# Gate and value products by Strassen's seven products for eight, with streamed weight sums, in a hashed attention and gated unit kernel

## The chip, the core and the metric

The kernel runs on one core of a Trainium2 chip. The metric is the device time of one execution in microseconds (us). It is 1079.8 us (median of three runs, 1078.91 to 1079.8) before the change. The core has five engines that run side by side, each through its own instructions in order: PE (TensorE, matrix products, whose results go to PSUM banks), DVE (VectorE), ACT (ScalarE), POOL (GpSimd) and SP, which here issues nearly all DMAs.

## The reference

```python
def _attn_ref(q, k, v, proj):                      # q, k, v: (4, 8, 768, 64)
    q_bits = (np.einsum('bhsd,dk->bhsk', q, proj) > 0).astype(np.int64)
    k_bits = (np.einsum('bhsd,dk->bhsk', k, proj) > 0).astype(np.int64)
...
    mask = q_bucket[:, :, :, None] == k_bucket[:, :, None, :]
    scores = np.where(mask, scale * np.matmul(q, k.transpose(0, 1, 3, 2)), -1000000000.0)
    attn = np.exp(scores - np.max(scores, axis=-1, keepdims=True))
    attn = attn / (np.sum(attn, axis=-1, keepdims=True) + 1e-09)
    return np.matmul(attn, v)

def _moe_ref(x, w_gate, w_val, w_out):             # x: (3072, 512); 512x1536, 512x1536, 1536x512
    gate = 1.0 / (1.0 + np.exp(-(x @ w_gate)))
    return gate * (x @ w_val) @ w_out
```

The output of the attention, with its heads side by side, is the `x` of the gated unit. The three weights come as 64-bit floats and are made into pairs of 32-bit numbers (a high part and a low part) on the chip.

## The kernel before

Every product of full precision is three matmuls: low by high, high by low, high by high. The tokens are eight units `(b, g)` of `GN` = 384 tokens: four batches, two halves each. The columns of gate and value are twelve blocks `j` of 128, the 512 rows of a weight four chunks `c`. One block of one unit takes 12 matmuls of 128x384 for the gate (tile `zg`), 12 for the value (`zv`), and then 9 matmuls of 128x512 into the three output tiles of the unit (`zo`, `yo`).

There are two stages. In the **attention stage** 16 pairs of heads go through scores (`sc`, L722 and L727), maximum (L736), exponential (L755), transposes (`tp`, L788), copies (`ef`, L795) and values (`pv`, L805); the result is stored to DRAM as `xd` (L818). Between these pieces PE does blocks 0 to 2 (`J1` = 3) of the six units of batches 0 to 2 (`moe_early`). At the same time 30 of the 36 weight blocks are loaded as raw 64-bit words and converted by DVE, ACT and POOL (`load_w`); 21 of them go back to DRAM (`kept`). When the last `xd` is stored, the task `switch` frees the attention's memory, and the **late stage** (`moe_late`) has all weights in SBUF: first batch 3 with all twelve blocks, then the other six units with blocks 3 to 11. A unit's `x` is loaded (`xr`) and split into `xh` (ACT) and `xl` (POOL or DVE); there is one buffer for it (`x=1`), so the split of the next unit waits for the last value product of the one before.

All instructions are tasks of a planner (`Plan`). It has a duration for each task, hands out buffers by counts (`stock`), and writes each engine's order down; on the chip each engine then goes through its order and waits only for data and buffers. A DMA's landing is planned as 2000 ns and 1 ns for 200 bytes, up to eight in flight without a common rate; the transfers after `switch` are planned with `CROWDED` = 1,600,000 bytes each in place of their own.

Of the kernel before, what the change touches and what calls it, by code (L numbers as in the profile page):

```python
# [169 lines left out]
def lsh_attention_glu_kernel(ctx, tc, q, k, v, proj, w_gate, w_val, w_out, out):  # L170
# [12 lines left out]
    J1 = 3  # L183
    J2 = 10
# [55 lines left out]
    hw = {}  # L240
    ALL = range(P // HB)
    for n, signs, groups in (("q", (1.0, -1.0), ALL), ("k0", (-1.0, 1.0), ALL[::2]), ("k1", (-1.0, 1.0), ALL[1::2])):
        w = const.tile([P, P], F32, name=f"hw{n}", tag="hw")
# [28 lines left out]
    def busy():  # L272
# [26 lines left out]
    def load_w(key, n, j, early, last=None):  # L299

        z = {}
        stage = lambda: later["w"] if last else stage1

        def load():
            z["raw"] = raw = stage().tile([P, 2 * N_EL], I32, name=f"raw{n}{j}", tag="wraw", bufs=2 if last else 1)
            if n == "o":  # L310
                nc.sync.dma_start(raw, w_out[j * P : (j + 1) * P, :])
            else:
                w = w_gate if n == "g" else w_val
                nc.sync.dma_start(
                    raw.rearrange("p (c f) -> p c f", c=KC),
                    w[:, 2 * j * P : 2 * (j + 1) * P].rearrange("(c p) f -> p c f", p=P),
                )
# [26 lines left out]
        def scaled(eng):  # L344
            eng.tensor_mul(f(z["ex"]), f(z["mf"]), f(z["ex"]))

        def high():
            if early or last:
                z["w"] = (w1 if early else stage()).tile([P, 2, N_EL], F32R, name=f"w{n}{j}", tag=f"w{n}{j}")
                weights[n, j] = z["w"][:, 0], z["w"][:, 1]  # L350
            else:
                z["w"] = stage1.tile([P, 2, N_EL], F32R, name=f"w{n}{j}", tag="wk", bufs=stock["wk"])
            nc.scalar.copy(z["w"][:, 0], f(z["ex"]))
# [580 lines left out]
```

## Time and profile before

| | us |
|---|---|
| median of three runs | 1079.8 |
| span of the profiled execution | 1077.3 |
| PE busy | 1056.2 (98%) |
| DVE busy | 556.1 (52%) |
| ACT busy | 493.0 (46%) |
| POOL busy | 261.1 (24%) |
| first late product | 579.0 |

The span is the time from the first to the last instruction. A matmul's busy time overlaps the next one's, since matmuls are pipelined; what one costs is the distance from its start to the start of the next. The profiled execution has no time of its own but its span; the median of the runs is 2.5 us above that span.

### The profile page before, as it was taken

To read this page: it belongs to the slowest core of one execution; us is meant where nothing else is said; L and a number is where in the kernel's file an instruction comes from. 1 tells how busy PE (TensorE), PEld (TensorE's weight loads), DVE (VectorE), ACT (ScalarE), POOL (GpSimd) and SP (SyncE) were. 2 spreads that over 40 slices of the span, in tenths; PEclk is the share of its full clock that TensorE was granted. 3 is DMA by queue.
4 is the path that set the end of the run, shared out by engine and by line. 5 is a ranking of instruction groups with operands and counts; after the bars stand their busy time and mean duration, and the time that the engine had idled before them with its cause. 6 is when DMAs were issued, how large, how long until landed. Compare 5 with 4: busy or idle time off the path is not lost.

```text
span 1077.3 us, 20491 instructions
## 1 busy us (share of the span) xinstructions
PE 1056.2 (98%) x8409; PEld 845.2 (78%) x8412; DVE 556.1 (52%) x1188; ACT 493.0 (46%) x887; POOL 261.1 (24%) x238
## 2 busy tenths in 40 slices
PE   9999999999999999999999999999999999999998
PEld 5665566677676776676678999999999999999997
DVE  6899899968788788788751181011021202020201
ACT  2867677767586676767652132112121212121211
POOL 0013233313324132323012172112121212121211
PEclk9999999999999999999999999999999999999999
DMA  8345545554664456443126621002020202020000
GB/s 206 84 125 159 148 148 138 160 162 129 197 199 127 156 154 192 149 143 135 56 61 248 267 80 59 1 1 88 1 88 1 89 1 89 1 83 6 31 28 30
DMA packets 110846, 113.54 MB, mean 105 GB/s; under 512 B 60320, under 2 KB 92064, under 8 KB 110752
## 3 DMA queue, kind: packets, MB, share of 16 engines
q1 hardware_dynamic: 110592, 112.23, 33.8%
q8 instruction: 66, 1.08, 0.4%
q14 instruction: 28, 0.23, 0.1%
q10 hardware_dynamic: 160, 0.00, 0.0%
HBM read 70.78 MB, written 28.84 MB: 92 GB/s over the span
## 4 chain that ended last, share of the span: by engine, by line
PE 83%; DVE 6%; ACT 4%; POOL 3%; DMA 2%; issue 2%; SPq 0%; POOLq 0%; DVEq 0%; ACTq 0%
PE pv L805 10%; PE sc L722 8%; PE zv_0l L429 8%; PE zv_1l L429 7%; PE zg_0l L429 7%; PE zg_1l L429 7%; PE yo_0l L462 7%; PE yo_1l L462 7%; PE tp L788 5%; PE zg L429 4%; PE zv L429 3%; PE zo L462 3%; PE sc L727 2%; DVE e L736 2%; ACT e L755 2%
## 5 line engine op out<-in xcount | busy, mean ns | idle before, releaser
L755 ACT ACTIVATE e<-e,st 128x768 f32<-128x768 f32 x192 | 196.4, 1025 | 81.2 <-DVE st L748 81.2
L736 DVE TENSOR_SCALAR_CACHE_REDUCE e<-sc 128x768 f32<-128x768 f32 x192 | 177.8, 952 | 34.9 <-PE sc L727 33.6
L805 PE MATMUL pv<-ef,vr 128*64 128x384 f32 x768 | 141.5, 497 | 0.0
L445 DVE TENSOR_TENSOR gf_1l<-zv_1l,sig 128x384 f32<-128x384 f32 x39 | 21.8, 558 | 208.6 <-PE zv_1l L429 208.6
L445 DVE TENSOR_TENSOR gf_0l<-zv_0l,sig 128x384 f32<-128x384 f32 x39 | 21.7, 557 | 189.8 <-PE zv_0l L429 189.8
L788 PEld LDWEIGHTS tp<-ident,e 64*128 64x128 f32 x2304 | 83.7, 139 | 30.5 <-issue 15.2
L795 DVE COPY ef<-tp 128x768 f32<-128x768 f32 x90 | 84.9, 951 | 26.1 <-PE tp L788 26.0
L788 PE MATMUL tp<-ident,e 64*128 64x64 f32 x2304 | 94.7, 226 | 2.4 <-ACT ef L795 1.0
L722 PE MATMUL sc<-kh,ql 64*128 64x384 f32 x192 | 86.2, 449 | 6.0 <-DVE ql L650 2.1
L795 ACT COPY ef<-tp 128x768 f32<-128x768 f32 x102 | 79.6, 792 | 25.3 <-PE tp L788 24.9
L805 PEld LDWEIGHTS pv<-ef,vr 128*64 128x64 f32 x768 | 47.8, 136 | 52.9 <-issue 46.5
L722 PE MATMUL sc<-kh,qsl 64*128 64x384 f32 x192 | 86.2, 449 | 3.1 <-ACT ef L795 1.1
L429 PE MATMUL zg_1l<-xh_1l,wg 128*128 128x384 f32 x312 | 86.4, 337 | 0.0
L429 PE MATMUL zg_0l<-xh_0l,wg 128*128 128x384 f32 x312 | 86.4, 337 | 0.0
L429 PE MATMUL zv_1l<-xh_1l,wv 128*128 128x384 f32 x312 | 85.5, 334 | 0.0
L429 PE MATMUL zv_0l<-xh_0l,wv 128*128 128x384 f32 x312 | 85.5, 334 | 0.0
L450 POOL TENSOR_TENSOR gl<-gf_1l,gh 128x384 fp32r<-128x384 f32 x39 | 40.5, 1039 | 184.5 <-ACT gh L449 184.5
L815 POOL TENSOR_TENSOR xs<-xs,rb 128x384 f32<-128x384 f32 x32 | 33.2, 1037 | 202.3 <-DVE xs L812 155.8
L450 POOL TENSOR_TENSOR gl<-gf_0l,gh 128x384 fp32r<-128x384 f32 x37 | 39.7, 1072 | 162.0 <-ACT gh L449 162.0
L462 PE MATMUL yo_0l<-wo,gh 128*128 128x512 f32 x234 | 73.5, 395 | 0.0
L462 PE MATMUL yo_1l<-wo,gh 128*128 128x512 f32 x234 | 73.5, 395 | 0.0
L581 ACT ACTIVATE sig<-zg_1l 128x384 f32<-128x384 f32 x39 | 19.2, 492 | 115.8 <-PE zg_1l L429 115.8
(160 smaller groups left out, 2495.0 us busy)
## 6 DMA issues: line engine op xcount, KB each, us to landing
kr<-in_k_dram SPq DMA_DIRECT2D x64, 96.0 KB
qr<-in_q_dram SPq DMA_DIRECT2D x32, 192.0 KB
vr<-in_v_dram SPq DMA_DIRECT2D x16, 384.0 KB
qsh<-qh SPq DMA_DIRECT2D x32, 192.0 KB
qsl<-ql SPq DMA_DIRECT2D x32, 192.0 KB
rb<-rd SPq DMA_DIRECT2D x64, 96.0 KB
xd<-xs SPq DMA_DIRECT2D x32, 192.0 KB
rawg<-in_moe_w_gate_dram SPq DMA_DIRECT2D x12, 512.0 KB
```

The source lines that it names most:

```text
L429: nc.tensor.matmul(z["acc"][:, :GN], a[:, wc], x[xx][:, c, :], start=(c == 0 and i == 0), stop=(c == KC - 1 and i == 2),)
L445: nc.vector.tensor_mul(z["gf"], z["acc"][:, :GN], sig[:, j])
L450: low = lambda eng: eng.tensor_sub(gl[:, j], z["gf"], f(gh[:, j]))
L462: nc.tensor.matmul(acc, a[:, slot, ts_], w, start=(first and i == 0), stop=(last and i == 2))
L722: nc.tensor.matmul(sc[:, j, :GN], q_[rows, c], z["k" + x][rows, h * GN : (h + 1) * GN], start=(m == 0), stop=False, tile_position=(j * D, 0),)
L727: nc.tensor.matmul(sc[:, j, :GN], z["qb"][rows, c], z["kb"][rows, h], start=False, stop=True, tile_position=(j * D, 0),)
L736: nc.vector.tensor_scalar(sp(e), gz["sc", t, h][:, :, :GN], -SCALE, None, op0=ALU.mult, op1=ALU.min, accum_out=gz["st", t][:, 0, h : h + 1],)
L755: nc.scalar.activation(e, e, AF.Exp, bias=st[:, 2, h : h + 1], scale=st[:, 1, h : h + 1], accum_out=gz["su"][:, h * GT + t : h * GT + t + 1],)
L788: nc.tensor.transpose(tp[:, r, at_ : at_ + D], gz["e", t, h][rows, c * P : (c + 1) * P], ident[rows, rows], tile_position=(r * D, 0),)
L795: copy(gz["ef", c].rearrange("p (n r d) -> p r n d", r=2, d=D), gz["tp", c][:, :, :GN].rearrange("p r (n d) -> p r n d", d=D),)
L805: nc.tensor.matmul(gz["pv"][rows, :GN], z["v"][:, h, c], gz["ef", c][:, h * GN : (h + 1) * GN], start=(c == 0), stop=(c == NC - 1), tile_p ...
L815: nc.gpsimd.tensor_mul(gz["xs"], gz["xs"], gz["rb"])
```

## The change

Gate and value columns are taken in pairs of blocks `jp`, and a whole batch (two units) at once. Of a pair, the two blocks of columns, the two halves of the 512 rows, and the two units of tokens make a 2x2 by 2x2 product, which Strassen's scheme (in Winograd's form) does with seven products in place of eight. `visit` is one gate or one value of one pair for one batch: seven times six matmuls of 128x384, in the order m1, m2, m6, m5, m7, m4, m3, in two PSUM banks. Bank B is read by ACT after m1, m6 and m7 while PE waits to add the next product to it (`copied`, tiles `t1`, `t16`, `t167`), and DVE adds those to the other bank (`summed`).

- The sums and differences of weights (`S1`, `S2`, `S3`, `S4`) are made once (`load_pair`), split, and kept in DRAM with the plain blocks: seven slices, two chunks and two parts, 1.835 MB for a visit. Each visit fetches them (`fetch_stream`) into one of three slots. The pairs 4 and 5 are converted in the late stage during the first batch.
- The sums of `x` are made at the beginning of each batch: tiles `x0` to `x6`, 128x768 each, with four differences (L649 of the changed kernel, tiles `rx` and `xb`), seven high parts on ACT (L654) and seven low parts (L657). Each has one buffer, released by the last visit of the batch before.
- The early blocks are now two (`J1` = 2), and all eight units do them; those of batch 3 come after the last `xd`, ahead of the visits. Ten of twelve blocks are in visits: 4 batches x 5 pairs x 2 = 40 visits.
- The output products of a pair are six pieces of six 128x512 matmuls; three go into each of the next two visits (`fill`).
- Each transfer is planned with its own size; `CROWDED` is unused.

```diff
-    J1 = 3
-    J2 = 10
+    J1 = 2
+    J2 = 8
+    JP1, JP2, JPN = J1 // 2, J2 // 2, NJ // 2
...
+    WS = 3
+    late_stock = dict(y=6, t=3, zt=3, xt0=1, xt1=1, ws1=1, ws2=1, xb=1, x1=1, x4=1, x5=1, x6=1)
...
+        def sums(eng):
+            y["f"] = full = f(z["all"]).rearrange("p (s m) -> p s m", s=SL)
+            at_ = lambda s_: full[:, s_]
+            eng.tensor_add(at_(S1), at_(A21), at_(A22))
+            eng.tensor_sub(at_(S2), at_(S1), at_(A11))
+            eng.tensor_sub(at_(S3), at_(A11), at_(A21))
+            eng.tensor_sub(at_(S4), at_(A12), at_(S2))
...
+        h0 = highs("x0", here("x0"), [l0])
+        t1 = differences("x4", "xt0", b12, here("x0"), [l0, lb])
+        ready["x0"] = lows("x0", here("x0"), [h0, t1])
+        t2 = differences("x5", "xt1", b22, diff("x4"), [t1])
+        h4 = highs("x4", diff("x4"), [t1], ["x4"])
+        ready["x4"] = lows("x4", diff("x4"), [h4, t2], ["xt0"])
+        t4 = differences("x6", "xt0", here("x1"), diff("x5"), [t2, l1, ready["x4"]])
+        h1 = highs("x1", here("x1"), [l1])
+        ready["x1"] = lows("x1", here("x1"), [h1, t4])
...
+            def mm(bank, a_, x_, first, last):
...
+                for c in range(2):
+                    for i, (wa, xa) in enumerate(((1, 0), (0, 1), (0, 0))):
+                        nc.tensor.matmul(
+                            acc, streams[n, jp][:, c, wa, a_], X[x_][:, xa, c],
+                            start=first and c == 0 and i == 0, stop=c == 1 and i == 2,
+                            skip_group_check=not first or not last,
+                        )
...
+            prev = m1 = m(prev, "B", A11, "x0", True, False, take=["one"], give=used("xr"))
+            e1 = copies("t1", m1)
+            prev = m2 = m(prev, "A", A12, "x1", True, True, take=["one"], give=used("x1"))
+            c11 = sum_(0, "A", "t1", [m2, e1], ["one", "t"])
+            prev = fill(prev)
+            prev = m6 = m(prev, "B", S2, "x5", False, False, [e1], give=used("x5"))
+            e16 = copies("t16", m6)
+            prev = m5 = m(prev, "D", S1, "x4", True, False, take=["one"], give=used("x4"))
+            prev = m7 = m(prev, "B", S3, "x2", False, False, [e16])
+            e167 = copies("t167", m7)
+            c22 = sum_(3, "D", "t167", [m5, e167], ["t"])
+            prev = fill(prev)
+            prev = m4 = m(prev, "B", A22, "x6", False, True, [e167], give=used("x6"))
+            prev = m3 = m(prev, "D", S4, "x3", False, True, [c22, *held], give=[slot_[1]] + used("x"))
+            c12 = sum_(1, "D", "t16", [m3, e16], ["one", "t"])
+            prev = fill(prev)
...
+        slots["last"] = dma(
+            1e3 + slots["n"], 1835008, fetch, after=[later["switch"], slots["last"], *keeps[n, jp]], take=[slot[1]]
+        )
...
-        made[w] = dma(1e3, CROWDED, fetch, after=[a, later["switch"]])
...
+        made[w] = dma(1e3 + w[1] * 2 - 2.5, 524288, fetch, after=[a, later["switch"]])
+    ends = dict(first=True, s=None, turn=0, pieces=[], sides=[dict(h=gh, l=gl, free=g_free[J1 - 1]), dict(free=None)])
+    prev = later["switch"]
+    for b in range(B):
+        prev = products(2e4 + b, b, prev, ends)
```

Where the stages meet, SP's order before was this (`xr` are the loads of `x`, `wg`, `wv`, `wo` the kept weights, `part` the stores of early sums):

```order
L818 DMA xd_65<-xs_3_1_8877 128x384
L364 DMA wg_8927<-kg_102 128x1024
L392 DMA xr_1l<-xd_65 128x4x384
L513 DMA part_100<-ob_2_1_8929 128x512
L364 DMA wv_8940<-kv_109 128x1024
L364 DMA wo_8948<-ko_116 128x1024
```

And it is this at the same place now (`wsg`, `wsv` are the streamed weights, `rawo` a raw output weight, `x_0` and `xb` the parts of `x` of batch 0):

```order
L486 DMA xr_1_8672<-xd_65 128x4x384
L1193 DMA wsg_40_8687<-kzg_108 128x3584
L406 DMA wo_8692<-ko_102 128x1024
L406 DMA wo_8699<-ko_103 128x1024
L406 DMA wo_8707<-ko_104 128x1024
L406 DMA wo_8712<-ko_105 128x1024
L406 DMA wo_8718<-ko_106 128x1024
L374 DMA rawo_8724<-in_moe_w_out_dram 128x1024
L406 DMA wo_8730<-ko_107 128x1024
L637 DMA x_0_8785<-xd_62 128x2x384
L642 DMA xb_8794<-xd_62 128x2x384 x2
L637 DMA x_0_8800<-xd_62 128x2x384
```

A fetch of 1.8 MB, six of kept output weights and one raw weight now stand between the last unit's `xr` and the first batch's `x`. On DVE the split of the first late unit before (`xl_0l`; `gf` are gatings, `exg` and `mfg` the first steps of a conversion) stood between two gatings:

```order
L795 COPY ef_3_1_5_8854<-tp_3_1_5_8835 128x2x6x64
L445 TENSOR_TENSOR gf_2_1_8869<-zv_2_1_8850,sig 128x384
L445 TENSOR_TENSOR gf_2_1_8893<-zv_2_1_8873,sig 128x384
L402 TENSOR_TENSOR xl_0l<-xr_0l,xh_0l 128x384 x2
L445 TENSOR_TENSOR gf_3_0l<-zv_3_0l,sig 128x384 x6
L323 TENSOR_SCALAR exg_9258<-rawg_9186 128x512
L330 TENSOR_SCALAR mfg_9264<-rawg_9186 128x512
```

Now the first step of the conversion of that raw weight (`exo`) stands inside the split of unit (3, 1), whose lows are `xl_1`, and the second raw weight's between the differences of batch 0 and its lows:

```order
L496 TENSOR_TENSOR xl_1_8751<-xr_1_8672,xh_1_8750 128x384
L324 TENSOR_SCALAR exo_8759<-rawo_8724 128x512
L496 TENSOR_TENSOR xl_1_8751<-xr_1_8672,xh_1_8750 128x384
L332 TENSOR_SCALAR mfo_8771<-rawo_8724 128x512
L538 TENSOR_TENSOR gf_3_0_8777<-zv_3_0_8735,sig 128x384
L337 SCALAR_TENSOR_TENSOR mfo_8771<-rawo_8724,mfo_8771 128x512
L342 SCALAR_TENSOR_TENSOR exo_8759<-rawo_8724,exo_8759 128x512
L649 TENSOR_TENSOR rx_0_8856<-xb_8794,x_0_8785 128x768
L649 TENSOR_TENSOR rx_0_8865<-xb_8794,rx_0_8856 128x768
L649 TENSOR_TENSOR xb_8794<-xb_8794 128x768
L324 TENSOR_SCALAR exo_8878<-rawo_8821 128x512
```

Between two batches (here 1 and 2) DVE before had only two lows of the next unit between its gatings:

```order
L445 TENSOR_TENSOR gf_3_0l<-zv_3_0l,sig 128x384
L450 TENSOR_TENSOR gl<-gf_3_0l,gh 128x384
L445 TENSOR_TENSOR gf_3_0l<-zv_3_0l,sig 128x384
L402 TENSOR_TENSOR xl_1l<-xr_1l,xh_1l 128x384 x2
L445 TENSOR_TENSOR gf_3_1l<-zv_3_1l,sig 128x384 x12
L402 TENSOR_TENSOR xl_0l<-xr_0l,xh_0l 128x384 x2
```

Now it has this (`rx`: differences; `x_2_10808`: low of `x4`; `x_2_10768`: low of `x1`; `zt` of L787: sums of PSUM banks; L846 and L848: gatings):

```order
L649 TENSOR_TENSOR rx_2_10795<-xb_10000,x_2_10756 128x768
L649 TENSOR_TENSOR rx_2_10806<-xb_10000,rx_2_10795 128x768
L787 TENSOR_TENSOR zt_1_10810<-zDv_1_10778,t167v_1_10803 128x384
L657 TENSOR_TENSOR x_2_10808<-rx_2_10795,x_2_10808 128x768
L649 TENSOR_TENSOR xb_10000<-xb_10000 128x768
L846 TENSOR_TENSOR zt_1_10832<-zBv_1_10740,sig 128x384
L787 TENSOR_TENSOR zt_1_10842<-zDv_1_10778,t16v_1_10785 128x384
L649 TENSOR_TENSOR rx_2_10844<-x_2_10768,rx_2_10806 128x768
L848 TENSOR_TENSOR zt_1_10842<-zt_1_10842,sig 128x384
L657 TENSOR_TENSOR x_2_10768<-x_2_10768 128x768
```

So the low part of `x1`, which m2 of the next batch reads, is the tenth of a row of DVE instructions that begins with the landing of `x0`.

More of the change, by code (lines that the diff above doesn't have):

```diff
@@ L297, in lsh_attention_glu_kernel, with floats, load_ @@
     fetches = []
-    def load_w(key, n, j, early, last=None):
+    def floats(key, load, after, last, name, other=False):
         z = {}
         stage = lambda: later["w"] if last else stage1
[L308 to L317, printed above, removed]
+        own = "2" if last else "1"
+        place = "xb" if other else "raw" + own
+        def load_():
+            tag = "xb" if other else "wraw"
+            z["raw"] = raw = stage().tile([P, 2 * N_EL], I32, name=f"raw{name}", tag=tag, bufs=1)
+            load(raw)
             pairs = raw.rearrange("p (n two) -> p n two", two=2)
@@ new lines, in floats, with load_w, load @@
+        d = add(key, "dve", 700, signed, after=[b2, c2], give=[place])
+        if other:
+            borrowed.append(d)
+        return z, add(key, "pool", 1300, scaled, after=[d]), own
+    streams = {}
+    keeps = {}
+    slots = dict(n=0, last=None)
+    borrowed = []
+    def load_w(key, n, j, early, last=None):
+        at_n = min(int(key), 90)
+        def load(raw):
+            if n == "o":
+                nc.sync.dma_start(raw, w_out[j * P : (j + 1) * P, :])
+            else:
+                w = w_gate if n == "g" else w_val
+                nc.sync.dma_start(
+                    raw.rearrange("p (c f) -> p c f", c=KC),
+                    w[:, 2 * j * P : 2 * (j + 1) * P].rearrange("(c p) f -> p c f", p=P),
+                )
+        z, e, own = floats(key, load, [last or score_tasks[at_n]], last, f"{n}{j}")
@@ L436, in product @@
                 key if c == 0 else OPEN, "pe", 3 * MM, lambda c=c: part(c), after=[prev, x["ready"][c], made[n, j], pace],
-                take=z["bank"] if c == 0 else [], give=["x"] if last and c == KC - 1 else [],
+                take=z["bank"] if c == 0 else [], give=(["x"] + (["ws0"] if last == "end" else [])) if last and c == KC - 1 else [],
             )
@@ L477, in moe_early @@
         for j in range(J1):
[L478 removed]
+            z, prev = product(key, u, "g", j, x, prev, False, next(pace))
             zs.append(add(
@@ L482, in moe_early @@
             ))
-        s_ = add(FIRST, "act", 3900, lambda: nc.scalar.activation(sig, sig, AF.Sigmoid), after=zs)
+        s_ = add(FIRST, "act", 3500, lambda: nc.scalar.activation(sig[:, :J1], sig[:, :J1], AF.Sigmoid), after=zs)
         ready = []
         for j in range(J1):
-            z, prev = product(key, u, "v", j, x, prev, j == J1 - 1, pace=next(pace))
+            z, prev = product(key, u, "v", j, x, prev, j == J1 - 1 and ("end" if ended else True), next(pace))
             z["gf_free"] = gf_last[0]
@@ L593, in lsh_attention_glu_kernel @@
+            ends["pieces"] += pieces(jp, side, done)
+            return prev
+        for jp, n in visits:
+            prev = visit(jp, n, (jp, n) == visits[-1], prev)
+        ends["first"] = False
+        return prev
     sp = lambda t: t.rearrange("p (j n) -> p j n", j=2)
```

417 lines of the change are left out of this document (298 added, 119 removed).

## The prediction

> **What bounds the kernel now.** The stretches come first, since they tell which engine is full where (columns: PE, PEld, DVE, ACT, POOL busy us, granted clock, DMA share, GB/s).
>
> ```profile
> 41.00:96.00 55.00, 53.90 (x652) 34.86 (x652) 49.78 (x119) 38.51 (x70) 9.18 (x8) 1.00 0.47 132
> 130.00:520.00 390.00, 383.22 (x3951) 271.31 (x3951) 318.24 (x702) 277.31 (x483) 118.24 (x101) 1.00 0.52 157
> 590.00:598.00 8.00, 8.00 (x45) 7.61 (x44) 0.56 (x1) 1.00 (x2) 1.01 (x1) 1.00 1.02 419
> 700.00:800.00 100.00, 99.67 (x520) 92.11 (x519) 15.71 (x23) 20.36 (x42) 21.39 (x20) 1.00 0.15 48
> ```
>
> In the late stage PE is full and DVE and ACT are at a fifth. In the attention stage (130 to 520) PE idles 6.8 of 390 us, though DVE is at 82%; from 41 to 96, ahead of any early product, DVE is at 91% and PE still idles only 1.1 of 55. Next the list of PE's waits from 20 to 545 us: its largest is 2.1 us.
>
> ```profile
> PE sc L722 <- DVE e L736: 2.1, 5, 0.7
> ```
>
> So PE's own work sets both stages, and products taken out of either shorten it. Their price is the distance of starts in the timeline of PE:
>
> ```profile
> 702.97 0.33 PE L429 MATMUL zg_1l<-xh_1l,wg 128*128 128x384 f32 x1
> ...
> 707.16 0.39 PE L462 MATMUL yo_1l<-wo,gl 128*128 128x512 f32 x1
> ...
> 709.24 0.33 PE L429 MATMUL zg_1l<-xh_1l,wg 128*128 128x384 f32 x1
> ...
> 544.55 0.44 PE L429 MATMUL zg<-xh,wg 128*128 128x384 f32 x1
> ...
> 546.85 0.96 PE L788 MATMUL tp<-ident,e 64*128 64x64 f32 x24
> ...
> 579.01 0.33 PE L429 MATMUL zg_0l<-xh_0l,wg 128*128 128x384 f32 x1
> ...
> 1073.01 0.61 PE L462 MATMUL yo_1l<-wo,gh 128*128 128x512 f32 x2
> ```
>
> 24 gate and value matmuls take 4.19 us (0.1746 each), nine output matmuls 2.08 (0.231 each); between attention pieces a block of 12 takes 2.30. The late stage runs from 579.0 to 1073.5; it holds 78 blocks of 24 and 9, 489.0 us at these prices, and 5.5 more at seven changes of unit.
>
> **The change, part by part.** The sum is made against the profiled span of 1077.3, and 2.5 us are added for the median of 1079.8.
>
> *Attention stage.* Each of six early units loses one block: 12 products of 12 at 2.30 (27.6 us) and 54 output matmuls at 0.231 (12.5). That is 40.1 us off 579.0. PE then has less to fill gaps with; it idled 6.8 us in 390, and I add 2 (bounds 0 and 12). Stage end: 540.9.
>
> *Late products.* 40 visits of 42 and two early units of 48 are 1776 matmuls of 128x384, 310.1 us; 720 and 36 output matmuls are 174.6. Together **484.7**, where 489.0 stood. Strassen's eighth thus nearly pays for the block that came over from the attention stage; the gain is taken there.
>
> *Inside a visit* PE waits for ACT's copies of bank B. Late rows show the chain of PE, DVE, ACT, POOL:
>
> ```profile
> 1062.32 0.33 PE L429 MATMUL zv_1l<-xh_1l,wv 128*128 128x384 f32 x1
> ...
> 1062.79 0.56 DVE L445 TENSOR_TENSOR gf_1l<-zv_1l,sig 128x384 f32<-128x384 f32 x1 [5.71 <-PE zv_1l L429]
> ...
> 1063.38 0.51 ACT L449 CAST gh<-gf_1l 128x384 fp32r<-128x384 f32 x1 [2.22 <-DVE gf_1l L445]
> ...
> 1063.97 1.01 POOL L450 TENSOR_TENSOR gl<-gf_1l,gh 128x384 fp32r<-128x384 f32 x1 [5.25 <-ACT gh L449]
> ```
>
> From the start of a product's last matmul DVE begins 0.47 later, and each hand-over takes 0.03 to 0.08. A copy by ACT is about 0.5, so bank B is free some 1.0 after m6's last start; m5 covers 0.17 + 1.05 = 1.22. After m1 and m7 a piece of 1.39 covers as well, and the sum for m3 (1.0 + 0.62) lies under a piece and m4 (2.6). Full visits cost nothing more. The first two have no pieces: m4 waits 0.8 in each, **+1.5**.
>
> *Streams.* A visit of 7.33 + 4.16 = 11.5 us needs 1.835 MB, 4.4 us at the 419 GB/s of the third row above, and three slots give it two visits. Hidden.
>
> *Sums of x between batches.* All tiles are single, so batch b+1's `x0` loads after m1 of the last visit. DVE rows show what two SBUF inputs cost, alone and beside POOL:
>
> ```profile
> 145.96 0.55 DVE L402 TENSOR_TENSOR xl<-xr,xh 128x384 fp32r<-128x384 f32 x1
> ...
> 572.16 2.32 DVE L402 TENSOR_TENSOR xl_0l<-xr_0l,xh_0l 128x384 fp32r<-128x384 f32 x2 [0.34 <-ACT xh_0l L399]
> ...
> 572.76 1.30 POOL L450 TENSOR_TENSOR gl<-gf,gh 128x384 fp32r<-128x384 f32 x1
> 574.03 1.33 POOL L402 TENSOR_TENSOR xl_0l<-xr_0l,xh_0l 128x384 fp32r<-128x384 f32 x1
> ...
> L650 DVE TENSOR_TENSOR ql<-tq,qh 128x768 fp32r<-128x768 f32 x16 | 15.1, 947 | 2.4 <-ACT qh L647 1.9 <-ACT wv L353 0.3
> ```
>
> 0.55 becomes 1.16: beside POOL, DVE goes at 0.47 of its pace. For 128x768 I take the last row, 0.95. The order puts ten DVE steps from the landing of `x0` to the low of `x1`: six of 0.95, a gating of 0.55, three of 0.56 from PSUM, 7.9 us alone. POOL has 7.1 us in that time (two lows of 768 at 2.0 by twice the 1.01 row, three of 384), which costs DVE 7.1 x 0.53 = 3.8: 11.7. When the load lands is an estimate from the last store, issued until 1074.71 and landed at 1077.3:
>
> ```profile
> 1073.02 1.69 SPq L547 DMA_DIRECT2D out_dram<-ob_1l  x3
> ```
>
> Of its 2.6 us its 0.26 MB are 0.6, so 2.0 pass around the data, say 1 ahead and 1 behind. A fetch of 1.835 MB issued 2 us before m1 of that visit goes first (data over at 1.0 + 4.4 - 2.0 = 3.4); the load's 0.39 MB take 1 and it lands at 5.4. PE reaches the next m2 after 11.7 (six more products, three pieces, m1). So m2 waits 17.1 - 11.7 = 5.4, and 0.6 is lost ahead of m3, whose sum stands behind the same differences. I take 6 for each of three boundaries, **+18**; the bounds are 1.8 each without POOL and 8.
>
> *Where the stages meet.* Let T be the end of the last values matmul (568.9 before).
>
> ```profile
> 567.37 1.51 PE L805 MATMUL pv<-ef,vr 128*64 128x384 f32 x8
> ...
> 572.70 0.32 SPq L364 DMA_DIRECT2D wg<-kg  x1
> ...
> 574.12 0.50 PE L462 MATMUL zo<-wo,gl 128*128 128x512 f32 x1 [1.57 <-POOL gl L450]
> ```
>
> The memory was free at T+3.8 (`wg`). Now `xr_1`, the stream, five kept weights and the raw weight come in this order: 0.79 + 1.84 + 2.62 + 0.52 = 5.77 MB, 13.8 us, and 2 around them: T+19.6. DVE's `exo` waits for it in the middle of unit (3, 1)'s split, and with 0.55 for it and for the low behind it that unit's third chunk is ready at T+20.7. PE has 12 output and 48 other matmuls, to T+11.2, idles about 2 for the split (the shared rows above), goes two chunks further (1.05) and idles 6.4, with the output matmuls of unit (3, 0) queued behind. Only now `x0`, which lies in `xr`'s buffer, can load, and `xb`, `x1` and the second stream after it; DVE's second `exo` waits for a raw weight behind these (3.93 MB and 2 around: T+32.1). Nine DVE steps, 6.3 us alone and some 1.5 for POOL's, bring the low of `x1` to T+39.9. PE, with 13.2 us of work from T+20.7, wants it at T+33.9. Idle 2 + 6.4 + 6.0, **+14** (the 1.6 us of the last row goes with the block removed). Bounds: 4, if the raw weights land early, and 20.
>
> *Conversions in the first batch.* Eight pairs of chunks and four output blocks are converted beside the visits, where POOL slows DVE. PE's stretch 130 to 520 had as many and idled 1.7%: of 115 us, 2. I take **+4** (0 to 10).
>
> *Tail.* 1077.3 - 1073.5 = 3.8 stays.
>
> Sum: 540.9 + 484.7 + 1.5 + 18 + 14 + 4 + 3.8 + 2.5 = **1069.4 us**, 1.0% under 1079.8: some 48 us of PE work go, 37 come back as waits.
>
> **Rivals.** *Hidden waits.* Landings come early enough and POOL's steps fall beside others: 4 at the meeting, 1.8 a boundary, 1 for conversions, 0 for filling. 540.9 - 2 + 484.7 + 1.5 + 5.4 + 4 + 1 + 6.3 = **1042**. For it: before, nothing but 1.6 us was lost there. Against it: `CROWDED` held late work back before, and the queue's bytes are plain.
>
> *A cold clock: slower.* The stretches at both ends show PE's clock follow its work:
>
> ```profile
> 2.00:7.25 5.25, 5.25 (x13) 1.95 (x14) 3.54 (x27) 1.83 (x3) 0.00 (x0) 1.00 0.88 214
> 1075.60:1077.30 1.70, 0.00 (x0) 0.00 (x0) 0.00 (x0) 0.00 (x0) 0.00 (x0) 0.51 0.18 70
> 2.00 7.28 PE L273 MATMUL idle<-sig 128*128 128x512 bf16 x21 [2.00 <-POOL sig L270]
> ```
>
> Of the 21 matmuls of the last row 13 touch the first 5.25 us, at 0.4 each, and eight fit into the 2.0 behind; at half the pace for that long a cold start costs some 2.5. At the end the clock was at half 2 us after the last matmul. If idle stretches over 2 us do this, the two at the meeting and one or two at each boundary add 5 to 8 x 2.5: **1084** (six). It decides where a boundary's wait passes 2 us in one piece; I expect 3.4 of the 6 in one piece. Against it: a cold PE also gives DVE time to catch up, so part is not paid. The Trainium skill, "TensorE: Matmul & The Clock Gate", section "What's actually happening", says that the clock falls to half after an idle window of about 3.4 us. By that rule only the meeting's stretches fall surely, +5; before, no gap in the trace was over 1.6, and the clock stayed at 1.00.
>
> *No gain in the attention stage.* DVE, at 82%, would become the bound there and POOL's larger conversions would stretch it; half of the 40 is lost: **1090**. Row 41 to 96 speaks against it.
>
> **How the numbers follow.** Forecast (1056 to 1077) 0.50; hidden waits 0.22; cold clock 0.17; attention stage or worse 0.11. The range 1043 to 1090 leaves out about 0.2. What a measurement here can tell from no change is 0.2%, 1077.6 to 1082.0. Of the forecast's 0.50, 0.04 is given to no change, and 0.05 of the slower cases too. Faster 0.22 + 0.46 = 0.68; same 0.09; slower 0.23.
>
> **What would show it.** Right: first unit (3, 0) product near 541; an idle PE of 6 us inside unit (3, 1) put down to DVE `xl`; one of 3 to 6 us at the first use of `x1` in batches 1, 2 and 3; 0.174 between starts inside visits. Wrong: waits for ACT's `t16` or `t167` in every visit (40 x 0.5 would be 20 us), waits for `ws` tiles, a clock below 1.00 in the late stage, or an attention stage that ends after 550.

## The result, and the profile after

The changed kernel takes 1096.5 us (median of four runs, 1095.4 to 1099.6) where the kernel before takes 1079.8 (four runs as well, 1078.9 to 1080.1): a ratio of 1.016, 95% interval 1.0146 to 1.0176. It is slower, and 27 us over the forecast. The profiled execution has a span of 1093.2 us, to be held against the forecast's 1066.9 (1069.4 less the 2.5 for the median).

First the busy times of the whole span, from the page of the changed kernel.

```profile
PE 1029.5 (94%) x8172; PEld 810.7 (74%) x8172; DVE 667.6 (61%) x1318; ACT 564.5 (52%) x1011; POOL 361.6 (33%) x336
```

PE is busy for 27 us less than the 1056.2 before, yet the span is 16 longer: PE, full before, now waits. The stretches of the changed kernel show where (columns: PE, PEld, DVE, ACT, POOL busy us with their instructions, granted clock, DMA share, GB/s).

```profile
130.00:495.00 365.00, 353.74 (x3780) 243.09 (x3778) 313.41 (x682) 263.48 (x457) 122.46 (x128) 1.00 0.54 165
545.90:584.00 38.10, 25.80 (x121) 21.98 (x120) 12.70 (x20) 15.12 (x28) 13.65 (x11) 0.85 0.90 338
584.00:610.00 26.00, 21.65 (x95) 18.84 (x96) 19.96 (x26) 12.37 (x23) 15.88 (x13) 0.82 0.65 228
...
622.70:714.90 92.20, 83.50 (x421) 73.81 (x420) 58.27 (x76) 38.14 (x69) 55.03 (x47) 1.00 0.53 190
...
721.00:836.00 115.00, 114.77 (x596) 106.34 (x596) 34.54 (x52) 37.31 (x74) 35.87 (x30) 0.99 0.53 188
836.00:841.00 5.00, 1.36 (x6) 1.03 (x5) 5.00 (x4) 2.55 (x5) 5.00 (x4) 0.79 0.69 295
...
1084.90:1093.20 8.30, 0.20 (x1) 0.00 (x0) 1.98 (x3) 0.00 (x0) 0.00 (x0) 0.69 0.42 136
```

Between boundaries (721 to 836) PE is full, as forecast. It idles where the stages meet (rows 2 and 3), beside the conversions of the first batch (row 4), at a boundary while DVE and POOL are full (row 6), and at the end (row 7). PE's list of waits (total, times, longest) names the same places:

```profile
PE zAg L772 <- DVE x L657: 12.0, 4, 3.6
PE zg L522 <- DVE xl L496: 7.5, 1, 7.5
...
PE zBg L772 <- DVE gf L538: 2.8, 1, 2.8
PE zBv L772 <- ACT t167v L780: 2.8, 2, 2.2
```

A visit is measured from the start of its first product (bank B) to that of the next visit. PE's timeline of the changed kernel gives a steady visit, a visit beside conversions and a boundary:

```profile
645.67 1.20 PE L772 MATMUL zBv<-x,wsv 128*128 128x384 f32 x6
...
659.86 1.21 PE L772 MATMUL zBg<-x,wsg 128*128 128x384 f32 x6
...
956.69 1.31 PE L772 MATMUL zBg<-x,wsg 128*128 128x384 f32 x6 [0.28 <-DVE zt L846]
...
973.63 1.21 PE L772 MATMUL zBv<-x,wsv 128*128 128x384 f32 x6
...
985.09 1.21 PE L772 MATMUL zBg<-x,wsg 128*128 128x384 f32 x6
```

985.09 - 973.63 = 11.46 is a full visit (42 matmuls and three pieces: 42 x 0.1746 + 18 x 0.231 = 11.5); 14.19 is one beside conversions, 16.94 one at a boundary. With such starts the 26.3 us between forecast and span come out as follows (us; a visit without pieces is 7.33, as in the prediction; the meeting runs from the first product of unit (3, 0) to the fourth visit of batch 0, the first batch from there over seven visits, a boundary over the first two visits of a batch, whose full length is 22.9).

| stretch | work in it | forecast | measured |
|---|---|---|---|
| attention stage, up to unit (3, 0) | | 540.9 | 545.9 |
| meeting | 51.2 | 66.7 | 76.9 |
| first batch, seven visits | 80.2 | 84.2 | 92.2 |
| three boundaries | 68.8 | 86.8 | 86.0 |
| from the start of the last matmul to the end | | 4.1 | 8.5 |

5.0 + 10.2 + 8.0 - 0.8 + 4.4 = 26.8; the steady visits between these stretches are 0.5 under the forecast.

### The profile page after: what moved, and what is told of

Its sections match the earlier page's. It is cut to its first block, busy times and chain, and to the rows that moved or that the text cites. A ratio compares the mean times of both kernels' runs of the same rounds, so it can differ in the third digit from the quotient of the medians.

```text
span 1093.2 us, 20583 instructions
## 1 busy us (share of the span) xinstructions
PE 1029.5 (94%) x8172; PEld 810.7 (74%) x8172; DVE 667.6 (61%) x1318; ACT 564.5 (52%) x1011; POOL 361.6 (33%) x336
## 4 chain that ended last, share of the span: by engine, by line
PE 70%; DVE 14%; ACT 5%; DMA 4%; issue 3%; POOL 3%; SPq 0%; DVEq 0%; POOLq 0%; ACTq 0%
PE y L555 13%; PE pv L1093 9%; PE sc L1010 8%; PE zBg L772 7%; PE zBv L772 6%; PE tp L1076 4%; PE zDg L772 4%; DVE e L1024 3%; PE zDv L772 3%; ACT e L1043 3%; PE zo L555 3%; PE zg L522 2%; PE sc L1015 2%; PE zAg L772 2%; DMA rawo<-in_moe_w_out_dram 2%
## 5 line engine op out<-in xcount | busy, mean ns | idle before, releaser
L555 PE MATMUL y<-wo,gh 128*128 128x512 f32 x480 | 152.5, 399 | 0.0
L848 POOL TENSOR_TENSOR zt<-zt,sig 128x384 f32<-128x384 f32 x50 | 57.1, 1143 | 240.6 <-DVE zt L787 240.6
L1076 PEld LDWEIGHTS tp<-ident,e 64*128 64x128 f32 x2304 | 85.2, 139 | 33.4 <-issue 14.8
L772 PE MATMUL zBg<-x,wsg 128*128 128x384 f32 x480 | 99.1, 341 | 7.0 <-DVE gf L538 2.8
L555 PEld LDWEIGHTS y<-wo,gh 128*128 128x128 f32 x480 | 91.3, 190 | 15.7
L772 PE MATMUL zBv<-x,wsv 128*128 128x384 f32 x480 | 97.0, 336 | 5.6 <-ACT t167v L780 2.8
L853 ACT CAST gh<-zt 128x384 fp32r<-128x384 f32 x80 | 41.0, 513 | 111.1 <-POOL zt L848 93.3
L772 PEld LDWEIGHTS zBg<-x,wsg 128*128 128x128 f32 x480 | 86.6, 191 | 14.8 <-DVE zt L846 4.1
L555 PE MATMUL y<-wo,gl 128*128 128x512 f32 x240 | 94.5, 394 | 0.0
L772 PEld LDWEIGHTS zBv<-x,wsv 128*128 128x128 f32 x480 | 85.0, 188 | 12.8 <-ACT t167v L780 3.9
L856 POOL TENSOR_TENSOR gl<-zt,gh 128x384 fp32r<-128x384 f32 x57 | 64.2, 1130 | 29.7 <-ACT gh L853 29.7
L832 ACT ACTIVATE sig<-sig 128x384 f32<-128x384 f32 x60 | 31.5, 526 | 67.1 <-DVE sig L787 67.0
```

The source lines that it names most:

```text
L555: nc.tensor.matmul(acc, a[:, slot, ts_], w, start=(first and i == 0), stop=(last and i == 2))
L772: nc.tensor.matmul(acc, streams[n, jp][:, c, wa, a_], X[x_][:, xa, c], start=first and c == 0 and i == 0, stop=c == 1 and i == 2, skip_gro ...
L848: eng.tensor_mul(w["z", blk], w["z", blk], sig[:, blk])
L853: nc.scalar.copy(side["h"][:, blk], w["z", blk])
L856: eng.tensor_sub(side["l"][:, blk], w["z", blk], f(side["h"][:, blk]))
L1076: nc.tensor.transpose(tp[:, r, at_ : at_ + D], gz["e", t, h][rows, c * P : (c + 1) * P], ident[rows, rows], tile_position=(r * D, 0),)
```

## The experiments

Most concern one place; the last two join what the others found. A diff shows only what is changed; "e2" stands for the edit of e2_all_early. Each kernel's ratio is to the kernel before, with its 95% interval.

**The attention stage.** e5_before_two is the kernel before with fewer early products and nothing else.

```diff
-    J1 = 3
+    J1 = 2
```

> The kernel before with two early blocks in place of three (J1 = 2) and no Strassen: the attention stage has the same early products as after the change, but before's conversions. The six units that are unwound early give 41.4 us of products (6 blocks by 6.9 us) to the late stage. Theory A (fewer products in the attention stage leave its waits uncovered): its last pv at 533 to 537 us, against 567.4 with three blocks less 41.4, that is 7 to 11 us lost; whole kernel 1087 to 1091 us. Theory B (the sums of weights and the larger conversions on GpSimd and VectorE lengthen it): last pv at 526 to 529 us, whole kernel 1080 to 1083 us.

1083.7 us, ratio 1.0036 (1.0023 to 1.0049). The last `pv` starts at 541.0 (after the change 542.6), the first product of unit (3, 0) at 544.2. The early products up to there took 124.4 us with three blocks and take 83.1 with two, so without loss it would be 579.0 - 41.3 = 537.7: 6.5 us are lost with no Strassen in the kernel, and 8.2 after the change; whether the 1.7 between them belong to the change stays open, since executions of one order differ by more (see the tail). One stretch shows how (columns as above; the kernel before, then e5_before_two):

```profile
130.00:495.00 365.00, 358.89 (x3715) 254.90 (x3713) 300.32 (x660) 263.33 (x458) 113.24 (x97) 1.00 0.52 157
```

```profile
130.00:495.00 365.00, 355.54 (x3820) 245.02 (x3818) 319.16 (x708) 268.35 (x472) 111.68 (x94) 1.00 0.56 172
```

PE idles 6.1, 9.5 and (after the change, above) 11.3 us; this stretch alone holds 3.4 and 5.2 us of the two losses. Theory A holds for the attention stage, whose last `pv` is even later than it said; its total was 3 us too high. The products taken out were also what filled PE while DVE, at 87% of this stretch for 82% before, caught up.

**The conversions in the first batch.** e2_all_early converts all blocks in the attention stage.

```diff
-    J2 = 8
+    J2 = 12
```

> All twelve blocks are converted in the attention stage (J2 = 12 for 8); nothing is converted in the first batch. Theory (the late conversions' instructions ahead of copies and sums in ScalarE's and VectorE's order cost 12 us of the first batch and 10 of the meeting): from the first late product to the end 15 to 20 us less, first batch without waits over 1 us; the attention stage takes 0 to 12 us more for twelve more conversions: 1078 to 1092 us. Rival (the first batch loses to the visits themselves or to the streams): its waits stay over 8 us, total 1096 or more.

1086.9 us, 1.0074 (1.0057 to 1.0092), within the expectation. The first batch of e2_all_early:

```profile
624.60:705.10 80.50, 80.33 (x421) 74.44 (x419) 20.58 (x32) 26.82 (x52) 27.14 (x23) 1.00 0.46 168
```

Seven visits in 80.6 us for 92.2, all but one at 11.46: the visits and their streams lose nothing, the conversions 12 us (11.6 by these two rows). The meeting gets 7.7 shorter; the attention stage gives 9.5 back. Why the conversions cost PE anything shows in the changed kernel's timeline of one visit:

```profile
651.59 1.19 POOL L444 TENSOR_TENSOR mfv<-mfv 128x128 f32<-128x128 f32 x1
...
654.90 0.94 ACT L456 CAST wsv<-mfv 128x896 fp32r<-128x896 f32 x1 [3.58 <-POOL mfv L447]
655.74 0.47 ACT L780 COPY t167v<-zBv 128x384 f32<-128x384 f32 x1
...
656.26 1.33 PE L772 MATMUL zBv<-x,wsv 128*128 128x384 f32 x6 [2.19 <-ACT t167v L780]
```

ACT stands 3.58 us before a conversion that waits for POOL, and behind it in ACT's order is the 0.47 us copy that PE needs. e12_prices and e13_conv_prices leave the work as it is and change the plan's prices, so that the order changes; the lines on `FIRST`, and a price of 1800 for 870 on the four differences of x, are e12's alone.

```diff
-[("dve", 900, lambda: sums(nc.vector)), ("pool", 1700, lambda: sums(nc.gpsimd))] if last
+[("dve", 1800, lambda: sums(nc.vector)), ("pool", 3600, lambda: sums(nc.gpsimd))] if last
...
-FIRST, [("dve", 870, lambda: low(n, of, nc.vector)), ("pool", 2000, lambda: low(n, of, nc.gpsimd))],
+FIRST, [("dve", 1800, lambda: low(n, of, nc.vector)), ("pool", 2600, lambda: low(n, of, nc.gpsimd))],
```

> The changed kernel with the prices of the late conversions and of the x parts in the plan set to what the traces show with both engines at work (sums 1800 and 3600 ns, low parts 1900 and 4200, x 1800 and 2600, GpSimd's product 2200). Only the order changes. Theory A (the order: ScalarE's copies for TensorE stand behind conversions that the plan thought done): the 11.9 us that the visits 5 to 9 of the first batch take over 11.46 each fall under 5: 1087 to 1090.5 us. Theory B (the load: VectorE and GpSimd have too much to do beside a visit): those 11.9 us stay above 8, total within 3 us of 1096.5.

> As e12_prices, but only the late conversions' prices in the plan are raised (sums 1800 and 3600 ns, low parts 1900 and 4200, GpSimd's product 2200); the x parts keep theirs. e12_prices took the visits 5 to 9 of the first batch from 11.9 us over 11.46 each to 5.0, and lost 11 us at the boundaries. Theory A (order: ScalarE's copies stood behind unfinished conversions): the first batch gains 5 to 9 us again and the boundaries stay at 16.7 to 18.0: 1087 to 1092 us. Theory B (the gain came from elsewhere, the boundaries lose with the conversions' order): within 3 us of 1096.5 or above.

e12_prices: 1104.5 us, 1.0229 (1.0205 to 1.0252), a miss in total. Its first batch takes 85.2 us, but the raised prices of x made the plan give `x1`'s low to POOL, behind gatings and splits there: PE waits 7.9, 6.7 and 7.8 us for it, and the boundaries grew to 32.5, 31.3 and 33.4. e13_conv_prices, without the x prices: 1090.8 us, 1.0101 (1.0086 to 1.0117), first batch 85.1, boundaries 29.0, 28.3 and 29.4. So 7 of the 12 us are an order, set by prices under what the steps take when both engines work; the other 5 were not taken apart.

**The boundaries: the clock.** e3_warm fills the gaps with dummy matmuls into a bank that the next product overwrites; they add work and change no result.

```diff
+    def warm(acc, n):
+        for _ in range(n):
+            nc.tensor.matmul(acc[:, :256], warm_[:, :P], warm_, start=True, stop=True)
...
+                    if (jp, n) == visits[0] and (bank == "A" if b else bank == "B"):
+                        warm(w[bank], 28 if b else 22)
```

> Dummy matmuls (128x256, 60 before the first zg of the last early unit, 22 before the first zBg, 28 before zAg of the first visit of batches 1 to 3) keep TensorE working inside the gaps that are there. Theory (half clock after a gap is a cost of its own on top of the waits): no stretch under 0.95 of the clock after the gaps of the boundaries, 2 us less at each of the last two, 4 at the meeting: 6 to 9 us less in all, 1087 to 1091 us, the waits themselves unchanged. Rival (only the waits count): within 2 us of 1096.5.

1095.9 us, 1.0146 (1.0131 to 1.0162): the rival's number. The same stretch in the changed kernel and in e3_warm, in this order (columns as above; the boundary begins at 835.1 in the one and at 837.1 in the other):

```profile
836.00:838.00 2.00, 0.63 (x4) 0.30 (x2) 2.00 (x2) 1.52 (x3) 2.00 (x2) 1.00 1.01 430
838.00:840.00 2.00, 0.00 (x0) 0.00 (x0) 2.00 (x2) 1.04 (x3) 2.00 (x3) 0.72 0.72 308
840.00:842.00 2.00, 1.73 (x5) 1.73 (x6) 2.00 (x3) 0.00 (x0) 2.00 (x2) 0.50 0.03 8
842.00:844.00 2.00, 2.00 (x6) 1.63 (x6) 2.00 (x1) 0.00 (x0) 1.57 (x1) 0.50 0.00 0
844.00:846.00 2.00, 2.00 (x8) 1.81 (x8) 1.53 (x3) 0.52 (x1) 0.00 (x0) 0.58 0.00 0
```

```profile
836.00:838.00 2.00, 1.44 (x8) 1.00 (x7) 2.00 (x4) 2.00 (x5) 1.46 (x1) 1.00 0.91 272
838.00:840.00 2.00, 2.00 (x20) 1.66 (x19) 2.00 (x2) 1.52 (x3) 2.00 (x2) 1.00 1.00 423
840.00:842.00 2.00, 1.63 (x15) 1.24 (x12) 2.00 (x2) 0.95 (x3) 2.00 (x3) 1.00 0.52 222
842.00:844.00 2.00, 1.80 (x9) 1.66 (x10) 2.00 (x3) 0.00 (x0) 2.00 (x2) 1.00 0.03 8
```

The clock is 1.00 in all of these rows, and yet the boundary is 1.0 us shorter here and none at the others (28.2 for 28.2, 28.2 for 28.4). DVE is full in the first four rows of either: a warm PE only comes sooner to the next wait. In e3_warm's list of waits the one on x is covered, 1.9 for 12.0, and one behind it has grown, from 1.0 to 4.3:

```profile
PE zDg L782 <- DVE sig L797: 4.3, 5, 1.1
...
PE zAg L782 <- DVE x L665: 1.9, 4, 0.6
```

The boundary that gained 1.0 had 6.8 us at half speed in the changed kernel (838.9 to 845.7), the two others 3.4 each. At the meeting e3_warm decides nothing: half speed falls from 20.5 to 6.8 us and the stretch stays at 77.1 for 76.9, but the 22 dummies there begin only when the wait for `gf` is over and hold the first visit up by 2.3 us.

**The boundaries: DVE and POOL.** e4_x_dve takes the low parts of x off POOL; e9_no_pool, on top of e2, the gates and splits too.

```diff
-FIRST, [("dve", 870, lambda: low(n, of, nc.vector)), ("pool", 2000, lambda: low(n, of, nc.gpsimd))],
+FIRST, "dve", 870, lambda: low(n, of, nc.vector),
```

> The seven low parts of x are all made on VectorE, none on GpSimd. Theory (VectorE's 768-wide operations take 2.0 to 2.6 us in place of 0.95 because GpSimd works on the same kind at the same time): they fall to about 1 us, and the three gaps of 3.8 to 4.0 us before zAg at the boundaries to under 2 us: 5 to 10 us less, 1086 to 1091 us. Rival (the chain is as long on one engine): seven lows and four sums by 1 us end no sooner, gaps 3 us or more, within 3 us of 1096.5.

1099.0 us, 1.0179 (1.0164 to 1.0194): slower, boundaries 31.3 to 31.5, the rival's number. But POOL still had gates and splits. The timeline of e4_x_dve:

```profile
826.99 1.01 POOL L855 TENSOR_TENSOR gl<-zt,gh 128x384 fp32r<-128x384 f32 x1 [0.62 <-ACT gh L852]
827.00 1.82 DVE L649 TENSOR_TENSOR rx<-xb,x 128x768 f32<-128x768 f32 x1 [1.73 <-DMA x<-xd]
...
828.92 0.96 DVE L657 TENSOR_TENSOR x<-x 128x768 fp32r<-128x768 f32 x1
```

0.96 alone, 1.82 when a POOL step of 1.01 began 0.01 earlier: nearly the sum. The Trainium skill, "SBUF — State Buffer", section "SBUF: two separate sides", says that a VectorE operation with two SBUF inputs and a GpSimd operation lock each other out for the whole instruction; this row agrees. If so, POOL's help is no help, which e9_no_pool tries.

> As e2_all_early, with the low parts of x, the gates and the splits of the products all on VectorE and nothing on GpSimd in the late stage. In e4_x_dve VectorE took 0.94 us for 128x768 while GpSimd was idle and 1.75 beside it, and GpSimd 1.01 and 1.67 for 128x384. Theory (the two together get no further than VectorE alone, so that GpSimd's share gains nothing): all of VectorE's 768-wide operations at 0.94 to 1.0, the three boundary visits 17.8, 16.9 and 18.0 fall by 1 to 4 us each: 3 to 12 us less than e2_all_early, 1075 to 1084 us. Rival (the work taken over from GpSimd fills what VectorE gains): the visits within 1 us of those, total within 3 us of 1086.9 or above.

1080.5 us, 1.0008 (0.9998 to 1.0017): boundaries 27.6, 25.6 and 27.1 where e2 has 29.2, 28.4 and 29.4. The theory holds: 6.8 us come with giving all of that work to the one engine. The three waits for x, 10.5 us in e2, are 7.5 here; most of the rest goes with the clock, since the boundaries have 6.8 us at half speed for 17.1 in e2.

**The boundaries: what PE has meanwhile.** e6_x_twice gives x0 and x1 of e2 a second buffer, so that they are made early. e10_held keeps e2's chain as it is and gives PE three out pieces to do there.

```diff
+        X0, X1 = ("x0b", "x1b") if b % 2 else ("xr", "x1")
```

> As e2_all_early, with a second buffer each for x0 and x1, so that the parts of x of the next batch are fetched, split and subtracted long before the boundary and only x4, x5, x2, x6, x3 remain for it. Theory (the chain from the freed x0 over VectorE's subtractions and splits to the first products sets the boundary, 17.8, 16.9 and 18.0 us in e2_all_early for a visit of 11.46): each of the three visits under 13 us, 13 to 18 us less than e2_all_early: 1069 to 1074 us. Rival (x4 to x3, or ScalarE's copies, end no sooner): visits of 15 us or more, less than 8 us gained.

```diff
+            if (jp, n) == visits[0]:
+                for _ in range(ends["lag"]):
+                    prev = fill(prev)
+                ends["lag"] = 0
             prev = m2 = m(prev, "A", A12, "x1", True, True, take=["one"], give=used("x1"))
```

> As e2_all_early, with three pieces of the out product (6 matmuls of 128x512, 1.39 us each) held back in each batch, by leaving out the filling piece at the end of three visits, and put between the first and the second product of the next batch. Theory (the boundary is a chain on VectorE, GpSimd and ScalarE of fixed length that TensorE waits out): the three boundary visits stay at 17 to 18.5 us although they hold 4.17 us more work, and 8 to 12 us go from the total: 1075 to 1079 us. Rival (the chain reaches past the second product, so the waits move behind it): visits of 20 us or more, less than 5 us gained.

e6_x_twice: 1090.7 us, 1.0096 (1.0080 to 1.0113), worse than e2. The first visit of a boundary falls to 14.8, but the one behind it grows to 13.1 at two of three: 28.0, 28.0 and 26.3 in all, 4.8 us under e2. The wait for x is gone; PE now waits in pieces of at most 1.4 us for DVE's sums and ACT's copies. The gain is lost elsewhere: the meeting is 7.3 us longer (and the attention stage, in the same order on DVE, ACT and POOL, 3.5). For 5.0 of the 7.3 the cause is in ACT's order:

```profile
607.00 0.83 ACT L656 CAST x<-x 128x768 fp32r<-128x768 f32 x1 [5.29 <-DMA x<-xd]
607.74 0.47 ACT L782 COPY t167g<-zBg 128x384 f32<-128x384 f32 x1
```

The high part of a second-buffer tile waits for its load, long before it is needed, and the copy that PE needs stands behind it. So e6 prices the second buffers together with a bad order.

e10_held (the pieces are left out of three visits of the batch before): 1072.0 us, 0.9936 (0.9920 to 0.9953), 15 us under e2 and 3 better than expected. Each boundary takes 28.25 with 4.17 us more work in it (27.09 in all), and the three batches that gave pieces away are 4 to 5 us shorter each. The chain needs its time; PE can use it.

**The meeting.** e1_crowded plans the late raw loads and kept weights as landing late, so that DVE's `exo` leaves unit (3, 1)'s split.

```diff
-a = dma(key, 524288, load_, after=after, take=[place])
+a = dma(key, CROWDED if last else 524288, load_, after=after, take=[place])
...
-made[w] = dma(1e3 + w[1] * 2 - 2.5, 524288, fetch, after=[a, later["switch"]])
+made[w] = dma(1e3 + w[1] * 2 - 2.5, CROWDED, fetch, after=[a, later["switch"]])
```

> The late raw loads and the six kept out-weight fetches are planned with the long landing time (1.6 MB) that the plan before used, so VectorE's first step on a late raw tile stands behind the splits and x sums of the meeting of the stages and no longer in the middle of them. Theory (the order on VectorE at the meeting costs the time): the gap of 7.83 us before zg of the last early unit falls under 1 us and the 3.11 us before the first zBg under 1.5 us, with the half clock there mostly gone: 8 to 14 us less, 1083 to 1089 us. Rival (the late landings themselves set the end: x parts sit in the same queue): the gap moves on to the first late products, within 2 us of 1096.5.

1099.4 us, 1.0180 (1.0165 to 1.0195), a miss. In the changed kernel the two DVE rows and PE behind them are

```profile
565.17 0.43 DVE L324 TENSOR_SCALAR exo<-rawo 128x512 int32<-128x512 int32 x1 [7.52 <-DMA rawo<-in_moe_w_out_dram]
565.51 0.55 DVE L496 TENSOR_TENSOR xl<-xr,xh 128x384 fp32r<-128x384 f32 x1
...
566.12 0.69 PE L522 MATMUL zg<-xl,we 128*128 128x384 f32 x1 [7.49 <-DVE xl L496]
```

In e1_crowded that gap is 0.7, and the meeting 71.4 for 76.9. But PE has long waits at two new places, both from its list of waits:

```profile
PE zo L555 <- DVE gl L543: 5.5, 2, 4.5
PE y L555 <- ACT wo L395: 5.4, 1, 5.4
```

The first is in the meeting itself: the second `gl`, for which PE waits 4.5 us, stands behind two steps of the x chain in DVE's order, of 2.1 and 2.6 us. The second: the last out weights, converted later, are late at the first boundary, 37.6 for 28.2. So moving the misplaced step won 5.5 us in the meeting, and cost 9.4 at the first boundary. The second raw weight does the same a little later: in the changed kernel DVE stands 6.3 us before its `exo`, `gf` comes behind it, and PE's first visit waits 2.8 for that.

e14_streams_first starts from e11_all (below), where no conversion is left and PE's list for 553 to 626 us is headed by

```profile
PE zBg L776 <- DMA wsg<-kzg: 5.3, 1, 5.3
...
PE zBg L776 <- DMA wo<-ko: 1.7, 1, 1.7
```

Ten kept out weights, issued together at the start of the late stage, stood ahead of that stream. The edit fetches each pair behind the stream of its value visit.

```diff
+                if ends["first"] and n == "v":
+                    for j in (2 * jp, 2 * jp + 1):
+                        a, fetch = pending["o", j]
+                        made["o", j] = dma(1e3 + slots["n"], 524288, fetch, after=[a, later["switch"], slots["last"]])
```

> e11_all with each pair of kept out weights fetched behind the stream of the value visit before it, in place of all ten at the start of the late stage. In e11_all TensorE waited 5.3 and 1.7 us for a stream and an out weight that landed late, with the 16 DMA engines full at 425 GB/s. Theory (5 MB of out weights at that rate, 12 us, stood ahead of the stream): those waits go, 4 to 7 us less: 1058 to 1061 us. Rival (VectorE's chain at the meeting ends as late): visits 1 and 2 stay above 13 us, total within 2 us of 1065.

1056.3 us, 0.9779 (0.9763 to 0.9795), 9 us under e11_all (6.4 by the spans) and 2 better than expected: the meeting takes 63.3 us for 70.8, and of the two waits 0.4 us is left.

**The tail.** e7_tail puts three of the last six early sums into tiles that are free by then.

```diff
+                    spare = ("xt0", "xt1", "xb")[t] if b == B - 1 and u == 1 else None
```

> The changed kernel with the last three early sums of the last batch fetched into the free tiles xt0, xt1 and xb, so that no fetch of an early sum waits for an output tile. Theory (the 8.3 us from the last matmul to the end are the wait for output tiles): 3.5 to 5 us less, 1091.5 to 1093 us, the last matmul unmoved. Rival (the last addition and store need that long by themselves): within 1 us of 1096.5.

1094.5 us, 1.0137 (1.0121 to 1.0153): 4.1 us from the start of the last matmul to the end for 8.5. Of these 4.4 the medians show 2.0, and the two spans 0.4, since the profiled execution came 4.0 later to its last matmul, 3.2 of them in the attention stage. DVE, ACT and POOL do the same in the same order there; at 320 us PE waits 2.5 us for 1.6, and the clock falls to half for 3.4 us, which it does not in the changed kernel. So a stretch differs by 3 us between executions without an edit of its own. In the changed kernel the last sum is fetched at 1086.40, after the last matmul, and added when it lands:

```profile
1086.40 0.38 SPq L719 DMA_DIRECT2D ob_3l<-part  x1
...
1089.57 0.69 DVE L715 TENSOR_TENSOR ob_3l<-y,ob_3l 128x512 f32<-128x512 f32 x1 [3.03 <-DMA ob_3l<-part]
```

**Together.** e11_all is e9_no_pool with the held pieces and the tail; e16_late_all joins the same, with e13's prices, to the changed kernel's eight blocks converted early.

> e9_no_pool (all blocks converted in the attention stage, nothing on GpSimd in the late stage) with the held pieces of e10_held and the tail of e7_tail. Theory: the three boundary visits at 15.7 to 17 us with 4.17 us more work in each, 7 to 10 us less than e9_no_pool, and 4 us less at the end: 1066 to 1070 us, faster than the kernel before (1079.8). Rival (what is saved at one place is waited out at the next): 1074 us or more.

> The changed kernel with its late conversions (J2 = 8) kept, their prices as in e13_conv_prices, the held pieces, the tail, and nothing of x, gates and splits on GpSimd. The attention stage ends 9.5 us sooner than in e11_all. Theory (each loss has its own place and they add): first batch 5 us over its visits, meeting as in the changed kernel, boundaries at 16 to 17 us with the held pieces: 1064 to 1071 us. Rival (the conversions on VectorE and GpSimd collide with what was moved to VectorE): 1074 us or more.

e11_all: 1065.0 us, 0.9870 (0.9856 to 0.9885). e16_late_all: 1064.5 us, 0.9856 (0.9842 to 0.9871). Both totals are as the theories said, e11_all's 1 us better: the losses had separate places, and their repairs add. The parts of e16_late_all are off both ways: its first batch loses 9 us over its work, not 5, and its meeting takes 71.1 us, not the 76.9 of the changed kernel. Each boundary of e11_all and e14_streams_first takes 27.07, its bare work. From e14_streams_first, the meeting, the first batch and a boundary:

```profile
556.50:619.80 63.30, 56.30 (x278) 50.11 (x278) 29.96 (x41) 29.65 (x55) 13.93 (x11) 0.95 0.82 305
619.80:695.80 76.00, 76.00 (x404) 71.26 (x403) 29.67 (x54) 26.85 (x52) 0.00 (x0) 1.00 0.59 219
695.80:722.90 27.10, 27.10 (x140) 24.77 (x139) 18.07 (x29) 9.41 (x17) 0.00 (x0) 1.00 0.58 197
```

PE is full from 619.8 on, and the kernel is 2.2% faster than before.

## Why the prediction was wrong

The sum had the right terms, and the late stage's work was right. Two of its signs came true, the 7.5 us put down to DVE `xl` and 3.5 to 3.6 us at the first use of `x1`. What failed are four sizes.

- **Products taken out of the attention stage, -40.1:** they were 41.3. The **2 us for lost filling** (bounds 0 to 12) measured 8.2; e5 shows 6.5 of them without any Strassen. The reading that failed is that a PE that idles little sets the pace by its own work: DVE at 82% was hidden by the very products that left.
- **Late products 484.7, streams hidden, 1.5 for visits without pieces:** right. Steady visits take 11.46, no wait in the changed kernel is put down to a stream, and two distances of 0.907 between starts, one in each of the visits without pieces, less 0.17 of work each, are the 1.5.
- **Boundaries, 3 x 6:** 17.2 in all. The chain was right: `x0` lands 3.4 to 5.8 us after the m1 that frees its buffer (forecast 5.4), the low of `x1` ends 11.6 to 12.5 after that (11.7), and m2 waits 3.5 to 3.6 in one piece (5.4). That the size agrees so well is partly luck: the waits at m2 make 10.6 of the 17.2, and some 5 (an estimate from the distances of starts) are matmuls at half the clock, which the sum put at nothing. Nor did it see that other waits stand close behind: with x0 and x1 there early (e6) a boundary stays at 26 to 28.
- **Meeting, 14:** 24 (76.9 - 51.2 - 1.5). The `exo` step in the middle of the split was forecast at 6.4, stands in the list of waits with 7.5, and taking it away won 5.5 (e1). By that list PE idles 17.1 us in the meeting, 1.2 of them in the visits without pieces: not far over the 14; what the sum lacked is about 5.5 us (the same kind of estimate) of matmuls at half the clock, and small losses after each wait. Conversions and the order of the queue are parts of it: without the former the meeting is 7.7 shorter (e2), and e14's order wins 7.5 of e11's 70.8. e14 still loses 10.6 by the same sum. How much a warm clock alone would win here stays open.
- **Conversions in the first batch, 4:** 12. The term was scaled from PE's idling in the attention stage. But a visit has ACT's copy in PE's own chain, covered by only 1.2 us of products after m6 and 1.6 after m7 by the prediction's own working, and one conversion ahead of it in ACT's order outlasts that. e13 shows 7 of the 12 to be order.
- **Tail, 3.8:** 8.3. The prediction kept the old tail and did not follow the new fetch of early sums into three output tiles.
- **The rivals.** The one nearest to the time (1090, no gain in the attention stage) is wrong in its reason: 33 of the 41 us were gained there. The cold clock's condition came true, 34 us at half speed in five stretches, but e3 took it away at the boundaries and won 1 us there, as the sentence against that rival had it; at the meeting it is not settled. (The longest gap before was 1.7 us, not 1.6.)

In sum, against e5, which has the same split of products: from unit (3, 0) to the last matmul e5 takes 534.1 us, 526.7 of them work at the prediction's prices (84 blocks of 6.27), and the changed kernel takes 538.8 for 484.7. Strassen took 42 us of products out, and what PE loses beside them rose from 7 to 54: 26 at the meeting, 12 in the first batch, 17 at the boundaries, less 1 in the steady visits. The late stage had been one long queue of products with nothing to wait for; it became visits with short chains through ACT and DVE.

## What to carry to other kernels

When products leave a full engine, ask of each stretch what they covered, not only what they cost: the second-busiest engine's share there is the warning. A plan orders by its prices, and an engine's order keeps a 0.5 us copy behind a 3.6 us wait: prices from rows in which the neighbours work too won 7 us with the conversions, but the same done to x sent a step to the slower engine and lost 11, so look at the order that comes out. And where a chain between stages cannot be shortened, hold back independent work for that place: here three pieces of 1.39 us at each of three boundaries were worth 15 us, while a warm clock was worth 1, second buffers 4.8 at the boundaries and a loss over all, and a second engine's help, taken away whole (e9), less than nothing.

## What the runs showed of the hardware

A DVE operation on two SBUF inputs and a POOL operation took each other's time in turn (0.96 us alone, 1.82 beside a POOL step of 1.01), and taking POOL's share over to DVE made the three boundaries 6.8 us shorter together (e9).

The clock fell sooner than after 3.4 us of idling. In the rows of the changed kernel under e3_warm PE stops at about 836.6; 0.72 in 838 to 840 is 1.12 of 2 us at half, so the fall is at 838.9, 2.3 us later, and 0.58 in 844 to 846 puts the return at 845.7, 6.8 us after it. The Trainium skill, "TensorE: Matmul & The Clock Gate", section "What's actually happening", has the clock fall after at least one idle window of about 3.4 us, in windows that run freely. The 6.8 us agree with two such windows; but the one before this fall, 835.5 to 838.9, had a third of its time at work. In e7_tail the clock fell at 321.9, when PE had stood still for 2.5 us; in the changed kernel PE stood 1.6 us at the same place and it stayed at 1.00. How long a fall lasted decided what a boundary took, 28.2 to 28.5 us with 3.4 at half speed and 29.0 to 29.5 with 6.8, in the changed kernel, e2, e7 and e13.
